# Which engine unpacks the low bits of float64 weights: GpSimd or ScalarE, chunks 3 to 15

## Chip, cores and metric

The kernel runs on one core of a Trainium2 chip. The metric is the device time of one execution in microseconds (us). Five engines work side by side, each through its own instructions in order: TensorE (PE in the profile, its weight loads PEld), VectorE (DVE), ScalarE (ACT), GpSimd (POOL) and SyncE (SP), which here only issues DMAs.

## What is computed

Attention over 8 batches, 8 heads, 576 positions and 64 channels, in which half of the heads see a local band of 32 positions and the other half every 32nd position, followed by a feed-forward layer with Gelu over the 4608 tokens:

```python
def _attn_ref(q, k, v):
    mask_local = (rel >= 0) & (rel < stride)                       # heads 0 to 3
    mask_strided = (rel >= 0) & (pos[None, :] % stride == pos[:, None] % stride)   # heads 4 to 7
    scores = np.where(masks[None, :, :, :], scale * q @ k.T, -1e9)
    return softmax(scores) @ v
...
def _moe_ref(x, w_in, w_out):          # x 4608x512, w_in 512x2048, w_out 2048x512, both float64
    h = x @ w_in
    g = 0.5 * h * (1.0 + erf(h * inv_sqrt2))
    return (g @ w_out).astype(np.float32)
```

The two weight matrices come as float64 and are handed to the chip as 64-bit words.

## The kernel before

The tokens are cut into 12 tiles of 384 (TT), the 2048 hidden channels into 16 chunks of 128 (NF). For each tile t and chunk f, `ffn_h` makes H (12 matmuls of 128x384, L598 to L600, from the tile's x in a high and a low float part and the chunk's weights w in two parts), `ffn_g` applies Gelu on ScalarE (L607), takes the high part gh on ScalarE (L609) and the low part gl on VectorE (L611), and `ffn_o` adds 9 matmuls of 128x512 into the three accumulators O (L637 to L639). In all 192 such steps; the first 16 (n below NB = 16) belong to tile 0.

Tile 0 cannot be worked on before its x is there (local attention L0 to L2, the strided attention of the jobs a, b and A) and before the chunk's weights have been loaded and unpacked. `load_w(f)` brings 1 MB, 128 rows of 1024 float64 words, into a tile ws (L133). `split_w(f)` then has six steps, which the list START names "c0" to "c15":

1. the low bits: byte 3 of each float64 word is shifted down by 5 bits and written as an integer over the low word (L146 on ScalarE as byte/32 - 0.49, rounded; L144 on VectorE for chunk 2);
2. the high word, read as a float, is scaled by 2^-112 (L152 on ScalarE; L150 on VectorE for chunk 10);
3. low = (high << 3) | low on VectorE (L154, two inputs from ws);
4. high = sign of high | low on VectorE (L156, two inputs from ws): now a float32;
5. its high part is copied to w[:, 0] (L160 on ScalarE; L162 on VectorE for chunk 9);
6. the rest goes to w[:, 1] on VectorE (L164, inputs from ws and w).

Only after step 6 may PE multiply by the chunk's weights. ws and w share a pool of 17 buffers of 8 KB per partition, so later loads wait until earlier chunks are through.

START is a list written out by hand: each entry takes one piece of one job (w = load, c = a step of split_w, f = a step of the feed-forward, L, a, b, A, u = attention pieces), and within the manual schedule around it VectorE, ScalarE, TensorE and SyncE run their instructions in just that order. GpSimd is not among the engines of that schedule; its instructions are ordered by the framework. After START, a loop over n = 16 to 193 (`step`) runs the other 11 tiles, in which VectorE works off the strided attention of the tiles to come.

What was on GpSimd before: the masks at the very start, one clearing of a 128x2048 tile (L765), and the small clearings of score tiles (L466).

Of the kernel before, what the change touches and what calls it, by code (L numbers as in the profile page):

```python
# [14 lines left out]
I32 = mybir.dt.int32  # L15
# [5 lines left out]
ALU = mybir.AluOpType  # L21
# [37 lines left out]
""".split()  # L59

LOW_V = [2]
EXP_V = [10]
HIGH_S = [0, 1, 2, 3, 4, 5, 6, 7, 8, 10, 11, 12, 13, 14, 15]
QUOT_V = (0, 2, 3)
# [19 lines left out]
def attn_ffn_kernel(ctx: ExitStack, tc: tile.TileContext, qk, vl, qka, va, qs, ks, vs, w, out):  # L84
    nc = tc.nc
# [41 lines left out]
    def slot(name, shape, dtype=F32):  # L127

        return wpool.tile(shape, dtype, name=name, tag="w")
# [5 lines left out]
    def split_w(f):  # L135

        raw = wst.pop(f)
        word = raw.bitcast(U32).rearrange("p (n two) -> p n two", two=2)
        high, low = word[:, :, 1], word[:, :, 0]
        byte = raw.bitcast(U8).rearrange("p (n e) -> p n e", e=8)[:, :, 3]  # L140
        hf = high.bitcast(F32)

        if f in LOW_V:
            nc.vector.tensor_scalar(low, low, 29, None, ALU.logical_shift_right)  # L144
        else:
            nc.scalar.activation(low.bitcast(I32), byte, AF.Copy, scale=1.0 / 32, bias=-0.49)  # L146
        yield

        if f in EXP_V:
            nc.vector.tensor_scalar(hf, hf, 2.0 ** -112, None, ALU.mult)  # L150
        else:
            nc.scalar.activation(hf, hf, AF.Copy, scale=2.0 ** -112)  # L152
        yield
        nc.vector.scalar_tensor_tensor(low, high, 3, low, ALU.logical_shift_left, ALU.bitwise_or)  # L154
        yield
        nc.vector.scalar_tensor_tensor(high, high, 0x80000000, low, ALU.bitwise_and, ALU.bitwise_or)  # L156
        yield
        wt = slot(f"w_{f}", [P, 2, 2 * DM], F32R)
        if f in HIGH_S:
            nc.scalar.copy(wt[:, 0, :], hf)  # L160
        else:
            nc.vector.tensor_copy(wt[:, 0, :], hf)  # L162
        yield
        nc.vector.tensor_tensor(wt[:, 1, :], hf, wt[:, 0, :].bitcast(F32), ALU.subtract)  # L164
        w1[f] = wt[:, :, 0:DM].rearrange("p t (c f) -> p t c f", c=NC)
        w2[f] = wt[:, :, DM:]
# [552 lines left out]
    def job(name):  # L719

        kind, x = name[0], int(name[1:])
        if kind == "c":
            yield from split_w(x)
        elif kind == "f":
            yield from ffn(x)
        elif kind in "ab":
            yield from half_tile(x, "ab".index(kind), sets[2]["ab".index(kind)])
        elif kind == "A":
            yield from strided_tile(x, sets[3])
        elif kind == "u":  # L730
            yield from unit_job([u for u in range(len(PLACE)) if PLACE[u][4] == x])
        else:
            yield from local_job(x, dve=x in QUOT_V, banks=sets[x == 1], pn=x if x < 2 else -1)
            if x >= JPT:
                load_jq(x + 3)
# [152 lines left out]
```

## Time and profile before

| | us |
|---|---|
| median of 3 runs | 902.62 (902.2 to 905.91) |
| the profiled execution | 902.33 |
| its span, first to last instruction | 900.6 |

Section 2 of the page shows where engines were busy in 40 slices of 22.5 us, 9 meaning 90% or more: PE is full from the third slice on, ScalarE is full only in the first four or five, VectorE nearly full through them and beyond. GpSimd (POOL) is idle after the first slice but for tiny pieces. Before the third slice PE waits for its inputs. "Lines" group instructions by source line, "waits" tell for what an engine stood idle, the "chain of waits" goes back from the last instruction to what released it.

### The profile page before, as it was taken

What the parts mean: (1) busy time and instruction counts of PE and PEld (TensorE: products, weight loads), DVE (VectorE), ACT (ScalarE), POOL (GpSimd) and SP (SyncE); (2) the same over time, 40 slices, a digit from 0 to 9 for tenths busy, and PEclk for the clock granted to TensorE, in tenths of its full rate; (3) what the DMA queues carried; (4) which work ended last, traced back from release to release, by engine and by line L of the source; (5) the groups of instructions that cost most, each with busy time, mean ns of one, the idle gap of its engine ahead of it and who ended that gap; (6) DMA issues with size and microseconds to landing.
All of it is one profiled execution on the core that took longest, in us unless ns stands there. A gap on an engine that the chain in (4) does not pass through costs nothing.

```text
span 900.6 us, 19161 instructions
## 1 busy us (share of the span) xinstructions
PE 869.3 (97%) x5948; PEld 772.4 (86%) x5948; DVE 716.2 (80%) x4894; ACT 443.5 (49%) x969; POOL 16.4 (2%) x86
## 2 busy tenths in 40 slices
PE   5599979999999999999999999999999999999998
PEld 4488868888888898888888888888888888889997
DVE  6899988787898899986998996988969899475110
ACT  6899643534544455445544445445453544443222
POOL 4000000000000000000000000000000000000000
PEclk9699998999999999999999999999999999999999
DMA  9992111312112112212121121113112200100001
GB/s 319 361 360 74 51 57 36 101 46 75 30 60 66 31 57 74 75 58 65 30 77 63 57 78 61 32 57 110 32 30 88 70 7 17 59 7 0 36 1 36
DMA packets 33399, 66.27 MB, mean 74 GB/s; under 512 B 6416, under 2 KB 15376, under 8 KB 31248
## 3 DMA queue, kind: packets, MB, share of 16 engines
q1 hardware_dynamic: 33296, 65.04, 22.2%
q8 instruction: 47, 0.77, 0.4%
q14 instruction: 56, 0.46, 0.2%
HBM read 51.64 MB, written 9.44 MB: 68 GB/s over the span
## 4 chain that ended last, share of the span: by engine, by line
PE 92%; ACT 3%; DMA 3%; SPq 1%; issue 0%; DVE 0%
PE H L598 15%; PE O L639 15%; PE O L638 15%; PE H L600 15%; PE H L599 14%; PE O L637 14%; PE X_L L324 2%; DMA ws<-in_w_dram 2%; PE S_L L287 1%; DMA vl<-in_vl_dram 1%; ACT w L160 1%; ACT ws L152 1%; ACT ws L146 0%; SPq L316 0%; ACT L607 0%
## 5 line engine op out<-in xcount | busy, mean ns | idle before, releaser
L607 ACT ACTIVATE H<-H 128x384 f32<-128x384 f32 x192 | 91.3, 476 | 374.5 <-PE H L600 347.3
L598 PE MATMUL H<-xh,w 128*128 128x384 f32 x768 | 264.3, 344 | 4.1 <-DVE gl L611 2.9
L599 PE MATMUL H<-xl,w 128*128 128x384 f32 x768 | 259.8, 338 | 0.7 <-DVE xl L233 0.7
L600 PE MATMUL H<-xh,w 128*128 128x384 f32 x768 | 260.4, 339 | 0.0
L515 DVE SCALAR_TENSOR_TENSOR acc<-sv,sc,acc 128x64 f32<-128x64 f32 x1158 | 248.3, 276 | 0.7
L639 PE MATMUL O<-w,gl 128*128 128x512 f32 x576 | 228.5, 397 | 0.0
L638 PE MATMUL O<-w,gh 128*128 128x512 f32 x576 | 227.8, 396 | 0.0
L637 PE MATMUL O<-w,gh 128*128 128x512 f32 x576 | 225.1, 391 | 0.0
L473 DVE CUSTOM_DVE_ANT_0 junk<-sq,sk 128x64 f32<-128x64 f32 x1290 | 204.3, 219 | 2.1 <-DMA sk<-in_ks_dram 2.1
L611 DVE TENSOR_TENSOR gl<-H,gh 128x384 fp32r<-128x384 f32 x192 | 105.6, 551 | 110.3 <-ACT gh L609 110.2
L598 PEld LDWEIGHTS H<-xh,w 128*128 128x128 f32 x768 | 145.4, 189 | 15.1 <-DVE gl L611 3.8
L599 PEld LDWEIGHTS H<-xl,w 128*128 128x128 f32 x768 | 145.6, 190 | 7.6 <-DVE xl L233 1.1
L600 PEld LDWEIGHTS H<-xh,w 128*128 128x128 f32 x768 | 145.5, 189 | 0.0
L639 PEld LDWEIGHTS O<-w,gl 128*128 128x128 f32 x576 | 108.3, 188 | 23.3
L638 PEld LDWEIGHTS O<-w,gh 128*128 128x128 f32 x576 | 108.4, 188 | 18.3
L637 PEld LDWEIGHTS O<-w,gh 128*128 128x128 f32 x576 | 108.7, 189 | 17.6
L473 DVE DVE_READ_ACCUMULATOR2_ANT sc<- 128x1 f32 x1290 | 106.4, 82 | 0.0
L609 ACT CAST gh<-H 128x384 fp32r<-128x384 f32 x192 | 92.2, 480 | 6.0
L607 ACT ACT_TABLE_LOAD x41 | 52.6, 1283 | 0.9 <-issue 0.2
L483 ACT ACT_TABLE_LOAD x35 | 44.9, 1283 | 0.6
L305 ACT ACTIVATE PT_L<-P_L,nm_L 128x64 f32<-128x64 f32 x120 | 39.9, 333 | 0.0
L231 ACT CAST xh<-X_L 128x256 fp32r<-128x256 f32 x30 | 11.2, 372 | 38.9 <-PE X_L L324 38.7
(106 smaller groups left out, 522.8 us busy)
## 6 DMA issues: line engine op xcount, KB each, us to landing
ws<-in_w_dram SPq DMA_DIRECT2D x16, 1024.0 KB, 14.8
qk<-in_qk_dram SPq DMA_DIRECT2D x36, 320.0 KB, 3.9
out_dram<-ob SPq DMA_DIRECT2D x34, 256.0 KB, 2.7
vl<-in_vl_dram SPq DMA_DIRECT2D x36, 192.0 KB, 2.8
sk<-in_ks_dram SPq DMA_DIRECT2D x8, 576.0 KB, 4.5
sv<-in_vs_dram SPq DMA_DIRECT2D x8, 576.0 KB, 3.8
band<-PT_L SPq DMA_DIRECT2D x240, 16.0 KB, 1.8
sq<-in_qs_dram SPq DMA_DIRECT2D x4, 576.0 KB, 3.6
```

Source lines behind the costliest of these rows:

```text
L473: nc.vector.tensor_tensor_reduce(junk, sq[vi, "q"][:, r0 + r, :], sq[vi, "k"][:, c, :], 1.0, 0.0, ALU.mult, ALU.add, ss[u][:, r, c:c + 1])
L483: exps.append((u, lambda: nc.scalar.activation(s, s, AF.Exp, scale=SC)))
L515: nc.vector.scalar_tensor_tensor(acc[:, r, :], sq[vi, "v"][:, c, :], wgt, acc[:, r, :], ALU.mult, ALU.add)
L598: nc.tensor.matmul(hp, w1[f][:, 0, c, :], xh[:, c, :], start=(c == 0), stop=False)
L599: nc.tensor.matmul(hp, w1[f][:, 0, c, :], xl[:, c, :], start=False, stop=False)
L600: nc.tensor.matmul(hp, w1[f][:, 1, c, :], xh[:, c, :], start=False, stop=(c == NC - 1))
L607: nc.scalar.activation(hp, hp, AF.Gelu)
L609: nc.scalar.copy(gh, hp)
L611: nc.vector.tensor_tensor(gl, hp, gh.bitcast(F32), ALU.subtract)
L637: nc.tensor.matmul(o, gh[:, sl], w2[f][:, 0, :], start=(f == 0), stop=False)
L638: nc.tensor.matmul(o, gh[:, sl], w2[f][:, 1, :], start=False, stop=False)
L639: nc.tensor.matmul(o, gl[:, sl], w2[f][:, 0, :], start=False, stop=(f == NF - 1))
```

## The change

For the chunks 3 to 15 the first step of `split_w` is made by GpSimd instead of ScalarE, with the same arithmetic (multiply by 1/32, add -0.49, rounded on writing an int32). Chunks 0 and 1 stay on ScalarE, chunk 2 on VectorE. All else is as it was.

```diff
 LOW_V = [2]
+LOW_P = [3, 4, 5, 6, 7, 8, 9, 10, 11, 12, 13, 14, 15]
 EXP_V = [10]
...
         if f in LOW_V:
             nc.vector.tensor_scalar(low, low, 29, None, ALU.logical_shift_right)
+        elif f in LOW_P:
+            nc.gpsimd.tensor_scalar(low.bitcast(I32), byte, 1.0 / 32, -0.49, ALU.mult, ALU.add)
         else:
             nc.scalar.activation(low.bitcast(I32), byte, AF.Copy, scale=1.0 / 32, bias=-0.49)
         yield
```

Line numbers behind the change are higher by 3: step 1 on ScalarE becomes L149, step 2 L155, step 3 L157, step 5 L163, Gelu L610.

ScalarE's rows before, at the place where the chunks 5, 6 and 4 are unpacked and tile 0's first H is waited for (ws_5_523 is the raw tile of chunk 5, PT_L2 and xh_0 are pieces of tile 0's attention and x):

```order
L146 ACTIVATE ws_5_523<-ws_5_523 128x1024
L152 ACTIVATE ws_5_523<-ws_5_523 128x1024
L257 COPY PT_L2_415<-S1_L2_413 96x512
L152 ACTIVATE ws_2_399<-ws_2_399 128x1024
L146 ACTIVATE ws_6_550<-ws_6_550 128x1024
L231 CAST xh_0_395<-S0_L2_412 128x2x128
L160 CAST w_1_584<-ws_1_371 128x1024
L152 ACTIVATE ws_6_550<-ws_6_550 128x1024
L146 ACTIVATE ws_4_561<-ws_4_561 128x1024
L160 CAST w_3_608<-ws_3_438 128x1024
L152 ACTIVATE ws_4_561<-ws_4_561 128x1024
L607 ACT_TABLE_LOAD
```

The same place on ScalarE now:

```order
L155 ACTIVATE ws_5_523<-ws_5_523 128x1024
L260 COPY PT_L2_415<-S1_L2_413 96x512
L155 ACTIVATE ws_2_399<-ws_2_399 128x1024
L234 CAST xh_0_395<-S0_L2_412 128x2x128
L163 CAST w_1_584<-ws_1_371 128x1024
L155 ACTIVATE ws_6_550<-ws_6_550 128x1024
L163 CAST w_3_608<-ws_3_438 128x1024
L155 ACTIVATE ws_4_561<-ws_4_561 128x1024
L610 ACT_TABLE_LOAD
```

Three instructions of 128x1024 are gone from before tile 0's first Gelu here; nothing else moved. The orders of VectorE, TensorE and SyncE are the same rows as before.

On GpSimd the thirteen new instructions stand in one piece behind the masks and ahead of the first clearings of the main loop:

```order
L147 TENSOR_SCALAR ws_3_438<-ws_3_438 128x1024
L147 TENSOR_SCALAR ws_5_523<-ws_5_523 128x1024
L147 TENSOR_SCALAR ws_6_550<-ws_6_550 128x1024
L147 TENSOR_SCALAR ws_4_561<-ws_4_561 128x1024
L147 TENSOR_SCALAR ws_12_586<-ws_12_586 128x1024
L147 TENSOR_SCALAR ws_9_606<-ws_9_606 128x1024
L147 TENSOR_SCALAR ws_7_644<-ws_7_644 128x1024
L147 TENSOR_SCALAR ws_14_658<-ws_14_658 128x1024
L147 TENSOR_SCALAR ws_15_694<-ws_15_694 128x1024
L147 TENSOR_SCALAR ws_8_717<-ws_8_717 128x1024
L147 TENSOR_SCALAR ws_11_806<-ws_11_806 128x1024
L147 TENSOR_SCALAR ws_13_830<-ws_13_830 128x1024
```

(Chunk 10 follows as the thirteenth.) That is the order in which SyncE issues the loads, not the order in which START calls for the chunks: each of the thirteen waits for its load only, so it runs when the chunk lands, where ScalarE's step 1 of the chunks 12 to 15 stood far later among other work.

## Prediction

> **What bounds the kernel now.** I read the page first, then the busy time in stretches of the start, then the waits of each engine there. Columns of the first rows: busy us, share of the span, instructions.
>
> ```profile
> PE 869.3 (97%) x5948; PEld 772.4 (86%) x5948; DVE 716.2 (80%) x4894; ACT 443.5 (49%) x969; POOL 16.4 (2%) x86
> PE 92%; ACT 3%; DMA 3%; SPq 1%; issue 0%; DVE 0%
> ```
>
> TensorE sets the end: 92% of the chain that ended last. What this change can reach is only when TensorE gets going, and whether it is kept fed while the chunks are unpacked. So to the stretches (columns: stretch, its length, then busy us of PE, PEld, DVE, ACT and POOL with counts, the granted PE clock, the DMA share and GB/s):
>
> ```profile
> 30.00:40.00 10.00, 6.62 (x46) 5.62 (x47) 7.56 (x8) 9.80 (x11) 0.00 (x0) 0.57 1.02 370
> 40.00:50.00 10.00, 7.71 (x33) 6.88 (x32) 9.38 (x20) 9.91 (x19) 0.00 (x0) 0.83 1.03 402
> 50.00:60.00 10.00, 9.53 (x63) 8.24 (x62) 10.00 (x41) 9.93 (x14) 0.00 (x0) 1.00 1.05 330
> 60.00:70.00 10.00, 10.00 (x63) 8.79 (x62) 9.95 (x21) 8.44 (x17) 0.00 (x0) 1.00 0.84 312
> ```
>
> ScalarE is full from 30 us to 60, VectorE from 50 on (and 9.4 of 10 before), GpSimd does nothing. TensorE is short of work until about 53 us and then full. Its only wait between 53 and 120 us is this one (columns: total, times, longest), and in the chain, in order of time, it comes out of ScalarE's row of pieces (start, us, what):
>
> ```profile
> PE S_L L264 <- ACT PT_L L257: 0.5, 1, 0.5
> ```
>
> ```profile
> 28.76 1.17 ACT ws L146
> ...
> 46.25 1.11 ACT ws L146
> ...
> 53.29 0.69 PE S_L L264 x16
> ```
>
> So ScalarE's step 1 lies on the path that starts TensorE; and from 53 us TensorE, VectorE and the hand-over between them are all tight at once. How tight, two rows of the order in time tell (start, us, engine line operation): the last step of chunk 8, and the first matmul that needs it.
>
> ```profile
> 74.58 1.23 DVE L164 TENSOR_TENSOR w<-ws,w 128x1024 fp32r<-128x1024 f32 x1 [0.42 <-ACT w L160]
> 76.41 0.33 PE L598 MATMUL H<-xh,w 128*128 128x384 f32 x1
> ```
>
> 74.58 + 1.23 = 75.81 against 76.41: **0.6 us of slack**. VectorE may come no later than that without TensorE standing still.
>
> **The change, part by part.** First what it removes. From the rows of the tile ws (ns: least, median, most; first and last start), with the loads and their time to landing:
>
> ```profile
> L133 SPq DMA_DIRECT2D ws<-in_w_dram x16: 327/328/635, 2.1 to 58.1; - x16
> L146 ACT ACTIVATE ws<-ws x15: 1109/1191/1265, 11.7 to 89.5; 128x1024 int32<-128x1024 uint8 x15
> DMA to landing us min/median/max: 7.2/14.8/18.1
> ```
>
> Thirteen of the fifteen L146 go, 13 x 1.19 = 15.5 us of ScalarE's time. Little of it reaches the end. Up to 53 us five of them go (chunks 3, 5, 6, 4, 7). Those of chunks 3 and 5 begin when their load lands, and step 2 then waits for the same landing, so each brings at most its own length. By the chain, the one at 28.76 brings forward what follows it by about 1.1 us, the one at 46.25 about as much; those between are partly lost because H of tile 0 also waits for xl from VectorE. I take 1.5 us (between 1.0 and 2.2) for TensorE's start. After 53 us ScalarE's relief meets a TensorE that is full, and is worth nothing.
>
> Then what it adds: thirteen TENSOR_SCALAR of 128x1024 on an idle engine, each starting when its chunk lands, between 24 and 69 us. They have time: GpSimd's order is the loads' order, the loads are (58.1 - 2.1) / 15 = 3.7 us apart, and VectorE has waited for a step 1 only once, 0.2 us (waits further down), though ScalarE mostly came to it later than the landing. So for GpSimd's own queue I charge nothing. The question is **what they do to VectorE**. Where GpSimd and VectorE ran together in the first 13 us, the trace has the answer. Rows in time, GpSimd's mask pieces of 32x64 beside VectorE's:
>
> ```profile
> 9.53 0.24 POOL L691 TENSOR_SCALAR_AFFINE_SELECT bmask<-bmask 32x64 f32<-32x64 f32 x1
> 9.54 0.64 DVE L224 TENSOR_TENSOR pbig<-pbig,rs_L 128x384 f32<-128x384 f32 x1
> ...
> 9.81 0.46 POOL L693 TENSOR_SCALAR_AFFINE_SELECT bmask<-bmask 32x64 f32<-32x64 f32 x1
> ```
>
> ```profile
> 11.01 0.35 DVE L379 TENSOR_TENSOR va<-va,Am 128x192 f32<-128x192 f32 x1
> 11.12 0.33 POOL L693 TENSOR_SCALAR_AFFINE_SELECT bmask<-bmask 32x64 f32<-32x64 f32 x1
> ```
>
> Undisturbed, the same two operations look like this (the second a row in time, the first from the groups by line: count, busy us, mean ns):
>
> ```profile
> L691 POOL TENSOR_SCALAR_AFFINE_SELECT bmaskNone<-bmaskNone 32x64 f32<-32x64 f32 x4 | 0.9, 232 | 0.2
> 25.74 0.54 DVE L224 TENSOR_TENSOR P_L<-P_L,rs_L 128x384 f32<-128x384 f32 x1
> ```
>
> VectorE's L224, with two inputs in SBUF, begins beside a running GpSimd piece and takes 0.64 instead of 0.54. GpSimd's next piece begins at 9.81 while L224 runs to 10.18, takes 0.46 instead of 0.23 and ends at 10.27; the one at 11.12 takes 0.33 and ends at 11.45, with VectorE's L379 having ended at 11.36. Twice GpSimd finishes 0.09 us after VectorE does. They do not share, **one waits for the other**. I take it that this holds for any GpSimd instruction that reads SBUF beside a VectorE instruction with two SBUF inputs.
>
> [...]
>
> How much of VectorE's time is open to it? Groups by line from 24 to 70 us, those with two SBUF inputs:
>
> ```profile
> L164 DVE TENSOR_TENSOR w<-ws,w 128x1024 fp32r<-128x1024 f32 x9 | 10.9, 1214 | 0.0
> L154 DVE SCALAR_TENSOR_TENSOR ws<-ws 128x1024 uint32<-128x1024 uint32 x9 | 10.9, 1221 | 3.0 <-ACT ws L152 2.9
> L156 DVE SCALAR_TENSOR_TENSOR ws<-ws 128x1024 uint32<-128x1024 uint32 x9 | 10.9, 1219 | 0.0
> L473 DVE CUSTOM_DVE_ANT_0 junk<-sq,sk 128x64 f32<-128x64 f32 x16 | 2.5, 222 | 0.0
> L420 DVE TENSOR_TENSOR xl<-qka,xh 128x192 fp32r<-128x192 f32 x4 | 1.7, 482 | 0.0
> L224 DVE TENSOR_TENSOR P_L<-P_L,rs_L 128x384 f32<-128x384 f32 x2 | 1.1, 548 | 0.0
> ```
>
> 10.9 x 3 + 2.5 + 1.7 + 1.1 = 38.0 of 46 us, 83%. Next, what one new instruction takes. The trace has none of its kind; the nearest rows on GpSimd (mean ns at the end):
>
> ```profile
> L765 POOL MEMSET band<- 128x2048 f32 x1 | 1.8, 1811 | 1.4 <-issue 1.4
> L342 POOL MEMSET va<- 128x512 f32 x1 | 0.5, 524 | 0.1
> masks.py:199 POOL TENSOR_SCALAR_AFFINE_SELECT ident<-ident 128x128 f32<-128x128 f32 x1 | 0.3, 293 | 0.1
> L685 POOL COPY mask<-mask 128x64 f32<-128x64 f32 x1 | 0.2, 236 | 0.0
> ```
>
> Below: the memset's slope, (1811 - 524) / 1536 = 0.84 ns per element, on the COPY: 0.236 + 960 x 0.84 ns = 1.04 us. Above: the 128x128 select taken eight times, 8 x 0.293 = 2.34 us. Between them the two selects, 32x64 at 0.232 and 128x128 at 0.293, give 0.95 ns per element and 0.293 + 896 x 0.95 ns = 1.15 us; the select is the nearest in kind (reads, computes, writes), so I take 1.2, and 1.3 with the 0.1 us that passing the turn cost above.
>
> [...] No row here shows a strided read on GpSimd.
>
> What VectorE can give back are its waits in that time (total, times, longest):
>
> ```profile
> DVE ws L154 <- ACT ws L152: 2.9, 2, 2.7
> DVE gl L611 <- ACT gh L609: 1.1, 1, 1.1
> DVE ss_L L215 <- ACT P_L L211: 0.4, 1, 0.4
> DVE w L164 <- ACT w L160: 0.4, 1, 0.4
> DVE ws L154 <- ACT ws L146: 0.2, 1, 0.2
> ```
>
> 5.0 us, all of them waits for ScalarE, which is now earlier. **The sum**: VectorE loses 13 x 1.3 x 0.83 = 14.0 us, has 5.0 back, and TensorE has 0.6 of slack at chunk 8: 14.0 - 5.0 - 0.6 = **+8.4 us**. The 1.5 us at TensorE's start are within it, since VectorE, not ScalarE, is then late. Behind 76 us TensorE was full, so a delay of that size is not won back; behind tile 0 everything waits for TensorE and shifts with it. With 1.04 us apiece (1.14 with the turn) the sum is 12.3 - 5.6 = +6.7; with 2.34 (2.44) it is 26.3 - 5.6 = +20.7.
>
> The profiled execution took 902.33 us (span 900.6 and 1.7 around it), 0.3 under the median of 902.62. 902.33 + 8.4 + 0.3 = 911.0.
>
> **Rivals.**
> - *GpSimd fits into the gaps.* If VectorE, issuing back to back, keeps its turn until an instruction with an input in PSUM comes (L611, 0.55 us; four L206, 0.7 us together), then each GpSimd piece lies beside some 0.5 us of such work and costs 0.8: 13 x 0.8 - 5.6 = +4.8, 907.4; with more of it in VectorE's waits, down to 903. For it: GpSimd waited twice at 9.8 and 11.1. Against: L224 waited too.
> - *No collision: not slower.* If integer and byte operands do not meet as the float ones above did, VectorE keeps its pace, and ScalarE's relief shows at the place where TensorE starts, the L264 at 53.29: -1.5, 901.1, at best -2.2. It decides if the L154, L156 and L164 beside GpSimd keep their 1.22 us. Against: the rows above, whose instructions differ only in type. That ScalarE's 15.5 us all reach the end would need a TensorE that waits behind 53 us, and it waits 0.5.
> - *The price is higher.* From 1.8 us apiece (strided bytes, two conversions) the loss is 13 x 1.9 x 0.83 - 5.6 = +14.9, 917.5, up to +20.7, 923.3. Beyond 3.7 us apiece, and sooner where loads lie closer, they would also queue up on GpSimd, whose order puts chunks 12 and 9 ahead of 7.
> - *The change does not do what it says*: a wait of ScalarE's step 2 for GpSimd, since both write the same tile, would put the thirteen back on ScalarE's path. Both touch different words; I give it nothing of its own.
>
> **How the numbers follow.** The forecast with its range of 906.5 to 916: 0.55. Gaps, 903 to 906.5: 0.12. No collision, 900 to 903: 0.13. Higher price, 916 to 923.5: 0.17. Something that makes it faster than -2.2: 0.03. The predicted time is 911.0. The range of 902.5 to 921 leaves out most of the no-collision case (0.11), the faster one (0.03) and the top of the dear one (0.04). About 0.5% (4.5 us) is what a measurement of this kernel can tell from no change. Faster by more: 0.03. Within it, up to 907.1: no collision 0.13, gaps 0.12, and 0.02 of the forecast, 0.27. Slower: 0.70.
>
> **What the changed profile would show.** Right: thirteen TENSOR_SCALAR on POOL between 24 and 80 us of 1.2 us or, where VectorE was first, longer; L154, L156 and L164 beside them up to 1.2 us longer than 1.22; VectorE without waits for ScalarE there; TensorE with several waits on VectorE (H on w, O on gl) between 44 and 80 us, 8 to 9 us in all, and nothing different behind 140 us. Wrong: L154 to L164 all at 1.22 (no collision), GpSimd pieces of 3 us and a VectorE without stretched rows (gaps), or TensorE's waits at other places, behind 80 us, for the x of tile 1.

## The result: 0.5% slower

| | before | with the change |
|---|---|---|
| median of 7 runs, us | 903.23 (902.2 to 906.62) | 908.87 (907.51 to 911.14) |
| the profiled execution, us | 902.33 | 907.51 |
| its span, us | 900.6 | 905.7 |
| ratio to before, 95% interval | | 1.0053 (1.0032 to 1.0074) |

The ratio stands for 4.8 us (2.9 to 6.7), the two profiled executions differ by 5.2. The forecast was +8.4 us, 911.0 in a range of 902.5 to 921.

### The profile after

The page's busy times and chain, as in the first rows of before:

```profile
PE 870.3 (96%) x5948; PEld 773.0 (85%) x5948; DVE 725.7 (80%) x4894; ACT 431.2 (48%) x956; POOL 35.6 (4%) x99
PE 90%; DMA 5%; DVE 2%; SPq 1%; ACT 1%; issue 0%; DVEq 0%
```

VectorE (DVE) has the same 4894 instructions and is busy 9.5 us longer (716.2 before). ScalarE is busy 12.3 us less. In the chain VectorE has taken the place that ScalarE had. The loads of ws have a larger share in it too, 5% where they had 2%, but VectorE waits for no load there, as shown below. A slower TensorE is not the reason either: its granted clock from 24 to 76 us was 0.83 before and 0.97 with the change. The rows of the tile ws (least, median, most ns; first and last start) say where most of the 9.5 us are, before and after:

```profile
L154 DVE SCALAR_TENSOR_TENSOR ws<-ws x16: 1208/1220/1228, 15.4 to 93.2; 128x1024 uint32<-128x1024 uint32 x16
L156 DVE SCALAR_TENSOR_TENSOR ws<-ws x16: 1207/1219/1224, 17.2 to 99.5; 128x1024 uint32<-128x1024 uint32 x16
L164 DVE TENSOR_TENSOR w<-ws,w x16: 1187/1218/1226, 23.0 to 104.5; 128x1024 fp32r<-128x1024 f32 x16
```

```profile
L157 DVE SCALAR_TENSOR_TENSOR ws<-ws x16: 1209/1218/2119, 16.4 to 97.9; 128x1024 uint32<-128x1024 uint32 x16
L159 DVE SCALAR_TENSOR_TENSOR ws<-ws x16: 1208/1215/2126, 18.2 to 104.3; 128x1024 uint32<-128x1024 uint32 x16
L167 DVE TENSOR_TENSOR w<-ws,w x16: 1194/1216/2122, 24.1 to 110.8; 128x1024 fp32r<-128x1024 f32 x16
L147 POOL TENSOR_SCALAR ws<-ws x13: 1100/1318/1986, 25.8 to 69.3; 128x1024 int32<-128x1024 uint8 x13
```

The medians are those of before; the longest are 0.90 us longer. Each of the thirteen GpSimd pieces stretched one VectorE instruction: eight by about 0.90 us, five by 0.19 to 0.59, 9.5 us together (eleven of them in these rows, one in an L423, one in an L476). One such place in the order of time (start, us):

```profile
39.03 1.21 DVE L159 SCALAR_TENSOR_TENSOR ws<-ws 128x1024 uint32<-128x1024 uint32 x1
40.17 2.11 DVE L167 TENSOR_TENSOR w<-ws,w 128x1024 fp32r<-128x1024 f32 x1
```

```profile
40.11 1.10 POOL L147 TENSOR_SCALAR ws<-ws 128x1024 int32<-128x1024 uint8 x1 [2.08 <-DMA ws<-in_w_dram]
```

GpSimd (POOL) begins 0.06 us ahead of VectorE's L167, takes 1.10 us undisturbed, and VectorE ends 0.90 us late. In the other order, GpSimd waits first and VectorE's next instruction after that:

```profile
35.85 1.21 DVE L167 TENSOR_TENSOR w<-ws,w 128x1024 fp32r<-128x1024 f32 x1
36.98 2.13 DVE L159 SCALAR_TENSOR_TENSOR ws<-ws 128x1024 uint32<-128x1024 uint32 x1
```

```profile
36.06 1.97 POOL L147 TENSOR_SCALAR ws<-ws 128x1024 int32<-128x1024 uint8 x1 [1.54 <-DMA ws<-in_w_dram]
```

TensorE's waits from 24 to 125 us (total, times, longest), before and after:

```profile
PE S_L L264 <- DMA vl<-in_vl_dram: 5.3, 1, 5.3
PE S_L L264 <- ACT PT_L L257: 4.5, 2, 4.0
PE H L598 <- DVE gl L611: 2.3, 1, 2.3
PE H L598 <- ACT xh L231: 1.3, 1, 1.3
PE H L599 <- DVE xl L233: 0.7, 1, 0.7
```

```profile
PE H L601 <- DVE gl L614: 7.2, 2, 4.0
PE S_L L267 <- DMA vl<-in_vl_dram: 4.9, 1, 4.9
PE H L602 <- DVE xl L236: 2.4, 1, 2.4
PE S_L L267 <- ACT PT_L L260: 1.9, 1, 1.9
PE S_L L258 <- DVE P_L L227: 0.8, 1, 0.8
PE H L601 <- ACT xh L234: 0.5, 1, 0.5
```

What TensorE waits for ScalarE fell from 5.8 to 2.4 us, what it waits for VectorE rose from 3.0 to 10.4. VectorE's own waits, 5.0 us from 24 to 76 us before, are gone: it waits for nothing up to 81 us.

### The profile page after: what moved, and what is told of

It is laid out like the page before. It is cut to its first block, busy times and chain, and to the rows that moved or that the text cites. A ratio compares the mean times of both kernels' runs of the same rounds, so it can differ in the third digit from the quotient of the medians.

```text
span 905.7 us, 19172 instructions
## 1 busy us (share of the span) xinstructions
PE 870.3 (96%) x5948; PEld 773.0 (85%) x5948; DVE 725.7 (80%) x4894; ACT 431.2 (48%) x956; POOL 35.6 (4%) x99
## 4 chain that ended last, share of the span: by engine, by line
PE 90%; DMA 5%; DVE 2%; SPq 1%; ACT 1%; issue 0%; DVEq 0%
PE H L601 15%; PE O L642 14%; PE O L641 14%; PE H L603 14%; PE H L602 14%; PE O L640 14%; DMA ws<-in_w_dram 5%; PE X_L L327 2%; PE S_L L290 1%; DVE ws L159 1%; SPq L319 0%; DVE w L167 0%; DVE ws L157 0%; SPq L187 0%; DMA band<-PT_L 0%
## 5 line engine op out<-in xcount | busy, mean ns | idle before, releaser
L610 ACT ACTIVATE H<-H 128x384 f32<-128x384 f32 x192 | 91.2, 475 | 384.9 <-PE H L603 356.0
L476 DVE CUSTOM_DVE_ANT_0 junk<-sq,sk 128x64 f32<-128x64 f32 x1290 | 204.1, 216 | 2.4 <-DMA sk<-in_ks_dram 2.4
L640 PEld LDWEIGHTS O<-w,gh 128*128 128x128 f32 x576 | 108.5, 188 | 17.6
L476 DVE DVE_READ_ACCUMULATOR2_ANT sc<- 128x1 f32 x1290 | 102.6, 80 | 0.0
L469 POOL MEMSET sc<- 128x16 f32 (+9 forms) x37 | 4.9, 135 | 680.2 <-DVE acc L518 680.2
```

The source lines that it names most:

```text
L476: nc.vector.tensor_tensor_reduce(junk, sq[vi, "q"][:, r0 + r, :], sq[vi, "k"][:, c, :], 1.0, 0.0, ALU.mult, ALU.add, ss[u][:, r, c:c + 1])
L610: nc.scalar.activation(hp, hp, AF.Gelu)
L640: nc.tensor.matmul(o, gh[:, sl], w2[f][:, 0, :], start=(f == 0), stop=False)
```

## The experiments

Theory A: a GpSimd instruction that reads SBUF and a VectorE instruction with two SBUF inputs hold each other up, and the time VectorE loses reaches the end. B: the loss is in ScalarE's shortened order or the loads. C: VectorE waits for low bits that come late. Times are medians; ratios are to runs of the kernel before on the same chip.

| run | step 1 of chunks 3 to 15 | median us | ratio (95%) | DVE busy us |
|---|---|---|---|---|
| before | ScalarE | 903.2 | 1 | 716.2 |
| the change | GpSimd | 908.87 | 1.0053 (1.0032 to 1.0074) | 725.7 |
| e1_none | left out | 898.75 | 0.9958 (0.9943 to 0.9973) | 716.5 |
| e2_twice | GpSimd, and a spare read each | 914.62 | 1.0134 (1.0117 to 1.0151) | 733.8 |
| e3_write_only | GpSimd, and a spare MEMSET each | 907.72 | 1.0062 (1.0045 to 1.0079) | 726.5 |
| e4_beside | ScalarE, and a spare GpSimd read each | 906.96 | 1.0041 (1.0026 to 1.0055) | 724.9 |
| e5_vector | VectorE | 906.61 | 1.0027 (1.0012 to 1.0042) | 723.7 |
| e6_two | GpSimd for 3, 5 | 902.74 | 0.9986 (0.9972 to 1.0) | 717.0 |
| e7_early | GpSimd for 3 to 7 | 902.28 | 0.9979 (0.9965 to 0.9993) | 719.3 |
| e8_late | GpSimd for 12 to 15 | 903.68 | 1.0002 (0.9987 to 1.0017) | 719.4 |
| e9_three | GpSimd for 3, 5, 7 | 901.32 | 0.9991 (0.998 to 1.0003) | 719.0 |
| e10_mixed | GpSimd 3, 5, 7; VectorE 4, 6 | 902.25 | 1.0005 (0.9995 to 1.0014) | 719.5 |

(In e6 to e10, ScalarE does the chunks not named.)

### Step 1 left out

```diff
+    zero = const.tile([P, 1], U32, name="zero")
+    nc.gpsimd.memset(zero, 0)
...
         elif f in LOW_P:
-            nc.gpsimd.tensor_scalar(low.bitcast(I32), byte, 1.0 / 32, -0.49, ALU.mult, ALU.add)
+            pass
...
-        nc.vector.scalar_tensor_tensor(low, high, 3, low, ALU.logical_shift_left, ALU.bitwise_or)
+        old = zero[:, 0:1].to_broadcast([P, 2 * DM]) if f in LOW_P else low
+        nc.vector.scalar_tensor_tensor(low, high, 3, old, ALU.logical_shift_left, ALU.bitwise_or)
```

> Step 1 of the chunks 3 to 15 is left out on every engine (their weights lack the three lowest bits; step 3 reads a zero column in place of the low word, still two SBUF inputs). Theory A, GpSimd and VectorE block each other: with no GpSimd piece L154, L156 and L164 are back at 1.22 us, ScalarE keeps its relief, and the time is 1 to 2 us under the kernel before, 901 to 902.5. Theory B, the loss comes from ScalarE's shortened order or the loads and not from GpSimd: it stays where the change is, about 908 to 909.

Measured: 0.9958, 3.8 us under the kernel before (2.4 to 5.1). VectorE's groups by line from 24 to 78 us:

```profile
L170 DVE TENSOR_TENSOR w<-ws,w 128x1024 fp32r<-128x1024 f32 x11 | 13.4, 1218 | 0.0
L160 DVE SCALAR_TENSOR_TENSOR ws<-ws,zero 128x1024 uint32<-128x1024 uint32 x10 | 12.2, 1220 | 0.0
L162 DVE SCALAR_TENSOR_TENSOR ws<-ws 128x1024 uint32<-128x1024 uint32 x10 | 12.1, 1218 | 0.0
```

All are at 1.22 us again. B falls: ScalarE's order is that of the change, the loads are issued in the same order, and the loss is gone. C falls already by the change's profile, in which VectorE waits for nothing from 24 to 81 us. This run also shows the relief by itself, and it is larger than both the 1.5 us of the forecast and the 1 to 2 expected here. From the change to this run lie 0.0095, 8.6 us, against 9.2 us of VectorE's busy time.

### A second piece beside each, reading or only writing

```diff
+    spare = const.tile([P, 2 * DM], U8, name="spare")
+    nc.gpsimd.memset(spare.bitcast(I32), 0)
...
             nc.gpsimd.tensor_scalar(low.bitcast(I32), byte, 1.0 / 32, -0.49, ALU.mult, ALU.add)
+            nc.gpsimd.tensor_copy(spare.bitcast(I32)[:, 0:1], low.bitcast(I32)[:, 0:1])
+            nc.gpsimd.tensor_scalar(spare, spare, 1.0, 0.0, ALU.mult, ALU.add)    # e2_twice
+            nc.gpsimd.memset(spare, 0)                                            # e3_write_only, in its place
```

The two comments say which run has which line. The one-column copy ties the second piece to the chunk's landing.

> The change, plus a second GpSimd TENSOR_SCALAR of 128x1024 (bytes of a spare tile, read and written) behind each of the thirteen, for which no other engine waits. Theory A: VectorE loses another 7 to 11 us, nothing is left for it to win back, and the time is 915 to 919. Theory C, the loss is VectorE waiting for low bits that GpSimd delivers late: the spare pieces push later ones back a little, 909 to 910.5, and no VectorE instruction is stretched more often than in the change.

> As the run with the second read, but the second piece is a MEMSET of the same spare tile, which writes and does not read. [...] Theory A', any GpSimd instruction blocks VectorE: as the second read, less what a MEMSET is shorter, 912 to 918.

With the second read VectorE is busy 8.1 us longer than in the change and the ratio rises by 0.0081, 7.3 us; the median of 914.62 is just under the 915 of A. C would have had 909 to 910.5, and falls with it. With the MEMSET, 1.0062 stands inside the change's interval, and the median of 907.72 is under the 912 to 918 of A', which falls. The tile spare of that run (least, median, most ns):

```profile
L151 POOL COPY spare<-ws x13: 205/1040/1192, 25.7 to 77.6; 128x1 int32<-128x1 int32 x13
L152 POOL MEMSET spare<- x13: 951/951/956, 26.1 to 78.0; 128x1024 uint8 x13
```

All thirteen MEMSETs take 0.95 us, and in the order of time one of them lies inside a VectorE instruction of two inputs that keeps its length:

```profile
38.07 1.21 DVE L164 SCALAR_TENSOR_TENSOR ws<-ws 128x1024 uint32<-128x1024 uint32 x1
...
38.25 0.95 POOL L152 MEMSET spare<- 128x1024 uint8 x1
```

So for VectorE's instructions with two inputs it was the reading that collided: VectorE is busy 726.5 us with the MEMSETs, 725.7 in the change and 733.8 with the second read (for a one-input instruction see the last section). The copies of a single column show the same from the other side: they read, and took 1.04 us in the median, up to a whole VectorE instruction of waiting, where an undisturbed one took 0.2.

### Blocking without relief

Against the kernel before, with LOW_P as in the change and spare as above:

```diff
         else:
+            if f in LOW_P:
+                nc.gpsimd.tensor_copy(spare.bitcast(I32)[:, 0:1], high.bitcast(I32)[:, 0:1])
+                nc.gpsimd.tensor_scalar(spare, spare, 1.0, 0.0, ALU.mult, ALU.add)
             nc.scalar.activation(low.bitcast(I32), byte, AF.Copy, scale=1.0 / 32, bias=-0.49)
```

> The kernel before, in which ScalarE keeps step 1, plus GpSimd's spare TENSOR_SCALAR of 128x1024 for each of the chunks 3 to 15 when it has landed (ScalarE waits only for a one-column copy ahead of it). Theory A: VectorE is stretched as in the change, thirteen times up to 0.9 us, and loses its waits for ScalarE in it, 907 to 911. Theory C: nobody needs the result, 903 to 904.

1.0041, 3.7 us: the loss comes back although nobody waits for GpSimd's result and ScalarE does all it did. No engine waits for spare in the profile. VectorE is busy 8.7 us longer, and of its 5.0 us of waits from 24 to 76 us 1.9 are still there. The 3.1 that are gone and 0.6 of slack leave 5.0 us, the upper end of the interval (2.3 to 5.0).

### Step 1 on VectorE

```diff
-LOW_V = [2]
-LOW_P = [3, 4, 5, 6, 7, 8, 9, 10, 11, 12, 13, 14, 15]
+LOW_V = [2, 3, 4, 5, 6, 7, 8, 9, 10, 11, 12, 13, 14, 15]
+LOW_P = []
```

> Step 1 of the chunks 3 to 15 on VectorE itself, as chunk 2 has it (0.69 us, 0.60 from start to start). With step 1 left out the kernel took 898.75 us, and all of VectorE's added time reaches the end: 13 x 0.60 = 7.8 gives 906.5, 905.5 to 907.5, under the change, whose thirteen pieces cost VectorE 9.5 us. Rival: VectorE, having nothing beside which to hide, loses more than to GpSimd, 909 to 912.

906.61 as expected, and VectorE is busy 7.2 us longer than with step 1 left out, against 9.2 in the change. By medians that is 2.3 us better than the change, though the two intervals overlap. VectorE loses no less by handing the work to GpSimd than by doing it itself.

### Some chunks only

Each is the change with a shorter list, `LOW_P = [3, 5]`, `[3, 4, 5, 6, 7]`, `[12, 13, 14, 15]`, `[3, 5, 7]`; the last also has `LOW_V = [2, 4, 6]`.

> Only the chunks 3 and 5 on GpSimd, the others on ScalarE. Their loads land ahead of VectorE's wait of 2.7 us for chunk 2 (29.7 to 32.4 us), so that wait takes up what the two pieces block, and ScalarE is relieved of two instructions ahead of tile 0's first H: 901 to 902.5. Rival, every GpSimd piece costs the end its 0.7 us wherever it lies: 903 to 904.5.

> The chunks 3 to 7 on GpSimd: the five whose step 1 stands on ScalarE ahead of 53 us. If the relief that leaving step 1 out showed (4.7 us) comes from these five, and each piece blocks VectorE for about 0.7 us, it is 903.4 - 4.7 + 5 x 0.73 = 902.4, 901 to 903.5. If the relief comes from all thirteen alike (0.36 each) it is 903.4 - 1.8 + 3.7 = 905.3, 904.5 to 906.5.

> The chunks 12 to 15 on GpSimd: their pieces run when they land, from 39 to 65 us, beside a full VectorE, while the ScalarE instructions they replace stood at 75 to 90 us beside a full TensorE. Blocking with no relief: 903.4 + 4 x 0.73 = 906.3, 905 to 907. If relief counts wherever it lies: 902 to 904.5.

> The chunks 3, 5 and 7 on GpSimd: 3 and 5 land ahead of VectorE's wait for chunk 2, and in the change the piece of chunk 7's neighbourhood at 42 to 45 us lay beside VectorE instructions with an input in PSUM. Three of the five early reliefs (4.7 x 3/5 = 2.8 us) for some 1 us of blocking that VectorE's waits take up: 900.5 to 902. If five early pieces already gave all there is: 902 to 903.

> The chunks 3, 5 and 7 on GpSimd, 4 and 6 on VectorE at 0.60 us each, the rest on ScalarE: all five early reliefs (4.7 us), 1.2 us of VectorE's own and about 1 us of blocking, part of which VectorE's waits take up: 899.5 to 901.5, under both kernels. If what blocks VectorE decides whatever its kind, as with five on GpSimd: 902 to 903.

Five early ones came out as the sum had it (902.28), and this is the one version with all bits that is under both kernels beyond its interval, by 0.2%. Two were as expected by ratio, 1.3 us under before, with an interval that ends at no change. The late four were a miss: VectorE is busy 3.2 us longer and the time is the same. The expectation had left out what the forecast's own sum had, that the first 5.6 us of blocking go into VectorE's waits and the slack; with that, 3.2 cost nothing. In this run's profile VectorE's waits from 24 to 76 us have fallen from 5.0 to 2.6 us. So this run doesn't show that relief counts late. Three chunks and the mixed version were misses by ratio (before took 901.66 on that chip), neither clearly under before: the reliefs do not add up chunk by chunk. The expectation for three had also taken the piece of chunk 7 for one beside inputs in PSUM; in the change that was chunk 9's, at 42.60, and chunk 7's, at 45.09, stretched an L167 to 2.10 us.

In the run with two, GpSimd's first piece met VectorE otherwise than in the change (two views, VectorE's rows and GpSimd's):

```profile
24.32 1.67 DVE L423 TENSOR_TENSOR xl<-qka,xh 128x192 fp32r<-128x192 f32 x4
25.91 0.55 DVE L227 TENSOR_TENSOR P_L<-P_L,rs_L 128x384 f32<-128x384 f32 x1
```

```profile
24.65 2.77 POOL L147 TENSOR_SCALAR ws<-ws 128x1024 int32<-128x1024 uint8 x1 [11.95 <-DMA ws<-in_w_dram]
```

VectorE went through five instructions at their usual length and GpSimd finished 0.96 us after the last. VectorE then had to wait for this chunk's low bits, which it does neither in the change nor in the other runs up to the late four, from 20 to 110 us:

```profile
DVE ws L157 <- POOL ws L147: 1.0, 1, 1.0
```

In the change, the same piece was let in between the second and the third L423, and the third took 1.40 us. What settles the turn is open; it wasn't tried.

## Why the prediction was right, and where its terms were off

- **The collision**: right, and shown by leaving the piece out, doubling it, making it write only, and running it beside for nobody.
- **What a piece takes**: forecast 1.2 us, between 1.04 and 2.34; undisturbed it took 1.10. The spare piece, with bytes side by side, took 1.04 at least, 0.06 less, so bytes 8 apart cost little. The 1.8 us of the rival with the higher price was a supposition that no run shows: the four pieces that took 1.76 to 1.99 us began beside a VectorE instruction and ended about 1.0 us after it.
- **What a piece costs VectorE**: this is the term that was mis-sized, 1.3 us where a stretched instruction shows 0.90 (2.12 against 1.22). VectorE loses 0.2 less than GpSimd takes (0.90 of 1.10; the cause was not tried apart), where I had added 0.1 for the hand-over. With 0.90 in its place the forecast's sum is 13 x 0.90 x 0.83 - 5.6 = +4.1 us.
- **The share of pieces that collide**: 83% forecast. 9.5 us of busy time are 13 x 0.90 x 0.81, but 0.81 is no share of pieces: all thirteen stretched something, eight in full. The five that in part ran beside inputs from PSUM cost 0.19 to 0.59, as the gaps rival said of such work: the cheapest, for chunk 9 at 42.60, stretched one L159 by 0.19 (1.40 us) behind four L209. That rival described a part of the pieces, not all. Its +4.8 is the measured number by coincidence: it came with no stretched rows.
- **What VectorE gives back**: 5.0 us forecast; all its waits there are gone.
- **Not won back later**: right. From 110.0 us before and 115.1 us after to the end, TensorE is busy 782.0 of 790.6 us in both.
- **The sum** with the measured terms: 9.5 - 5.0 - 0.6 = 3.9 us. Measured 4.8 by ratio (2.9 to 6.7). The profiled pair differs by 1.3 more. VectorE was already 1.0 us behind ahead of GpSimd's first piece at 25.79 (before, then after):

```profile
24.14 1.68 DVE L420 TENSOR_TENSOR xl<-qka,xh 128x192 fp32r<-128x192 f32 x4
25.17 2.57 DVE L423 TENSOR_TENSOR xl<-qka,xh 128x192 fp32r<-128x192 f32 x4
```

The run with the MEMSET, which has the change too, is there at 24.22, so the change alone does not bring this delay. Whether that 1.0 us reaches the end is not shown.
- **The relief of ScalarE**: forecast 1.5 us, at best 2.2; without a collision it is 3.8 (2.4 to 5.1). VectorE's waits from 24 to 76 us fall with it from 5.0 to 1.6, and I had counted only TensorE's start. It did not enter the sum. The forecast had no collision at 901.1 as a rival; that would have come out faster still.
- **Where it would show**: TensorE's new waits on VectorE stand at 35.98 (2.4 us), 47.99 (4.0) and 67.59 (3.2); the first lies ahead of the 44 to 80 us named. In all TensorE waits 10.4 us for VectorE, where 8 to 9 were forecast, and none of it is H waiting for w or O for gl: it is H waiting for gl and xl, and a matmul on P_L.

## What to carry to other kernels

An idle engine is no free engine where its reads and those of a busy one hold each other up: before moving work to GpSimd beside a full VectorE, look which VectorE instructions read two inputs from SBUF, and charge them nearly the piece's own length (here 0.90 us of 1.10). Count in first what the waiting engine can give back. In the five runs that added work for all thirteen chunks (the change, the second read, the MEMSET, blocking without relief, step 1 on VectorE), VectorE's added busy time, 7.5 to 17.6 us, was 4.7 to 5.5 us more than the time added by ratio (busy time from one profile each): about that much was free, and the rest came through. With fewer chunks moved it was 2.1 to 5.0. A mixed result of relief and collision is taken apart by leaving the moved work out and by doing it twice.

## What the runs showed of the chip that was not expected

A VectorE instruction with one small SBUF input was held up too. In the run with blocking but no relief (VectorE's row, then GpSimd's):

```profile
47.93 1.00 DVE L222 TENSOR_SCALAR ss_L<-ss_L 128x4 f32<-128x4 f32 x1 [0.19 <-ACT P_L L218]
```

```profile
47.87 1.04 POOL L152 TENSOR_SCALAR spare<-spare 128x1024 uint8<-128x1024 uint8 x1
```

GpSimd began 0.06 us earlier. The same TENSOR_SCALAR on four columns takes 0.17 us in the median before.

A one-input instruction was held up by a piece that only writes, too. In the run with the MEMSET (VectorE's row, then GpSimd's):

```profile
71.25 1.21 DVE L170 CAST w<-ws 128x1024 fp32r<-128x1024 f32 x1
```

```profile
70.96 0.95 POOL L152 MEMSET spare<- 128x1024 uint8 x1
```

This CAST takes 0.68 us before and in the change. The MEMSET ended at 71.91 and the CAST 0.55 us later. It is one row; no run was made for it.

And GpSimd was passed over for long: its piece took 2.77 us in the run with two and 3.48 in the run with the five early chunks, where an undisturbed one took 1.10.
